# Attention with a token mixer: the value products of two steps in one burst, behind the eighth slot of a pair

## The chip, the cores and the metric

The kernel runs on one core of one Trainium2 chip. The metric is the device time of one execution in microseconds. The engines are named as the profile names them: PE (TensorE, matrix products; PEld is its load of the stationary operand), DVE (VectorE), ACT (ScalarE), POOL (GpSimd) and SP (SyncE, here a queue of transfers). PE writes into PSUM, which has eight banks; a bank holds 128 rows of 512 numbers. Each engine works its instructions off in the order of the program and waits, where it must, on semaphores.

## The reference

From one input x of 2048 tokens by 512 channels, normalised over the channels to xn, two branches are computed and joined:

```python
def _A_ref(x, wqkv, wo):
    H = 32; Dh = D // H                      # 32 heads of 16
    q, k, v = ...                            # x @ wqkv
    p = _softmax(einsum("bhqd,bhkd->bhqk", q, k) * Dh ** -0.5)
    return einsum("bhqk,bhkd->bhqd", p, v)...reshape(B, S, D) @ wo

def _B_ref(x, w1, b1, w2, b2):
    h = _layernorm(x)
    u = _gelu(einsum("bsd,sf->bdf", h, w1) + b1)     # F = 1792
    return (einsum("bdf,fs->bds", u, w2) + b2).transpose(0, 2, 1)

xn = _layernorm(x)
out = x + _A_ref(xn) * _silu(_B_ref(xn))
```

The softmax is over all 2048 keys, so for each of the 32 heads there are 2048 by 2048 scores, their row maxima, their exponentials and the products with the values.

## The kernel before, in words

A first part (to about 200 us of the span) normalises x, makes q, k and v and puts them away in device memory. Then comes the main loop, which this change is about.

**Steps.** The heads are taken in 16 pairs. For a pair of heads there are 32 steps of scores: a step `t` is one block of 128 keys against one span of 1024 queries, for both heads (`a` = 0 and 1, in rows 0 to 63 and 64 to 127 of PE) and both halves of the span, so four products of 512 columns (`score`, L750), each followed by an exponential on ACT that writes a `prob` tile (L762). The values of a step (`values`, L764) are four products with the `prob` tiles, which stand side by side in four column groups of PE; in the trace a step has eight instructions for them, all of L773. They add up in the one bank `av` over the 16 blocks of keys. When the last is done, `put_away` (L509) is put on a list: ACT copies `av` out and SP sends it away.

**Maxima.** The exponentials need the row maxima beforehand. So a second stream runs 20 steps ahead (`LEAD`): `max_of` (L378) multiplies 128 queries by 512 keys, and DVE reduces the bank to one column (L391). There are four such products a step as well, two for either head. Once in 16 steps the maxima are complete for a span; `max_rows` (L393) takes the negative, PE turns it (`turn`, L402), DVE and POOL copy it, and four transfers of POOL's queue write it into rows of q.

**The mixer.** The token mixer's matrix products (48 products of 512 columns for a tile of the first matrix, 42 for one of the second, all into the one bank `dn`) are fed in between. Each is cut into two halves of 64 rows (L911), so that a half runs beside a product of the attention in the other half of the rows. When a tile is complete, ACT reads `dn` (`gelu`, L459, or `silu`, L493), and the next tile may begin.

**Banks.** Three banks are for scores (`sc`), three for maxima (`mx`), one is `av`, one is `dn`.

**The order in a pair of steps.** The loop (L944) does two steps at a time, `s` and `s + 1`. It takes up to six products of the mixer and follows an order written out by hand (`ORDERS`, L892): two strings, one for either half of PE's rows, in which `m` is a maximum, `s` a score and `D` a half of a product of the mixer. Position i of the two strings is a slot: its two products run side by side. The strings have 8, 10, 12 or 14 slots, for 0, 2, 4 or 6 products of the mixer; this document calls that the kind of the pair. In kind 6 the maxima are in slots 0, 2, 4, 6, 7, 9, 11 and 13 and the scores in 1, 3, 5, 6, 7, 8, 10 and 12. The third entry of an order is the slot ahead of which the loop stops: there it turns the maxima if that is due, emits the values of step `t - 2` (L969), and works off the list of later work (`run_later`). The values of step `t - 1` are emitted after the last slot (L1020). So PE does two bursts of values in a pair: one in the middle, one between the pairs. A tile of the mixer that ends within a pair leaves a shorter take, and the next pair begins the next tile with kind 4.

**The list of later work.** `later` holds functions; `run_later` runs them all, at the top of a pair and at its middle; `after(n, f)` runs f at the n-th time.

**The tail.** After step 492 of the scores there are no maxima left, and PE does the output's products (L886) between the scores. For the last heads' first span, `own` (L606) makes two pieces of work for the side; the second, `move_in` (L641), divides the values and sends them by POOL's queue into rows of `oc`. From the block of tokens number eight on, `rest` (L781) waits for `own_done` before it emits a product that reads those rows (L816).

Of the kernel before, what the change touches and what calls it, by code (L numbers as in the profile page):

```python
# [21 lines left out]
def tile_attention_token_mixer(ctx, tc, x, wqkv, wo, w1, b1, w2, b2, out):  # L22
# [343 lines left out]
    def after(n, f):  # L366

        later.append(f if n == 1 else lambda: after(n - 1, f))
# [232 lines left out]


    asides = []
    own_done = [False]

    def own(span, ev):  # L606
        rq = sm.tile([P, 4, 4], F32, name="rq", bufs=1)
        wide = el.tile([P, 512], F32, name="t", bufs=4)

        def one(pl=ps_mx, nm="mx"):  # L610

            ps = pl.tile([P, 512], F32, name=nm)
            for k in range(4):
                at = slice(k * P, (k + 1) * P)
                nc.tensor.transpose(ps[:, at], ev[:, at], ident)
            turned = ps.rearrange("p (k j r) -> p k j r", k=4, j=4)
            for a in range(2):
                nc.vector.reciprocal(rq[:, :, 2 * a : 2 * a + 2], turned[:, :, 2 * a : 2 * a + 2, 16 - 16 * a])
            nc.vector.tensor_copy(
                wide.rearrange("p (k j r) -> p k j r", k=4, j=4), rq.unsqueeze(3).to_broadcast([P, 4, 4, 32]),  # L620
            )

        def two(pl=ps_mx, nm="mx"):

            ps = pl.tile([P, 512], F32, name=nm)
            for k in range(4):
                nc.tensor.matmul(
                    ps[:, k * P : (k + 1) * P], wide[:, k * P : (k + 1) * P], ident, start=True, stop=True,
                )
            return ps  # L630

        def chunk(ps, of, at):
            nc.vector.tensor_tensor(out=ev[:, at], in0=ps[:, at], in1=ev[:, at], op=OP.mult)
            nc.scalar.copy(of[:, 0, at], ev[:, at])
            sub(nc.vector, of[:, 1, at], ev[:, at], of[:, 0, at])

        if span == QH - 1:
            asides.extend((one, two, chunk))
            return

        def move_in():  # L641
            ps = two()
            of = el.tile([P, 2, 512], F32R, name="uo")
            chunk(ps, of, slice(0, 512))
            for a in range(2):
                for c in range(2):
                    row = 32 * (2 * a + c) + DH * a
                    move(oc[ND - 1, c][96 + DH * a : 112 + DH * a, :, :], of[row : row + DH, :, :], nc.gpsimd)
            own_done[0] = True

        asides.extend((one, move_in))


# [110 lines left out]
    def values(t):  # L764
        p, r = divmod(t, SPP)
        span, kb = divmod(r, NB)
        if kb == 0:
            state["av"] = ps_av.tile([P, 512], F32, name="av")
        av = state["av"]
        for a in range(2):  # L770
            for c in range(2):
                j = 2 * a + c
                nc.tensor.matmul(  # L773
                    av[32 * j : 32 * j + 32, :],
                    vps[p][:, kb, 16 * a : 16 * a + 32], prob.pop((t, a, c)),
                    start=kb == 0, stop=kb == NB - 1,
                )
        if kb == NB - 1:
            later.append(lambda: put_away(p, span, av))

    def rest():  # L781

        for n in range(N_W - 2, N_W):
            w_split(n)
        for b in range(2):
            load_part(b)

        def until(ready):
            while not ready():
                yield None  # L790

        def products(ps, b, groups, rows=None):
            at = slice(b % 4 * P, (b % 4 + 1) * P)
            for g in groups:
                o = oc[g, b // 4]
                at_g = rows if g == ND - 1 else None
                for j, (m, w) in enumerate(((0, whs), (0, wls), (1, whs))):
                    w = w[N_MIX + g].rearrange("p a b -> p (a b)")
                    yield (
                        ps, lambda r, o=o, m=m, s=at_g: o[s or r, m, at], lambda r, w=w, s=at_g: w[s or r, :],  # L800
                        g == groups[0] and j == 0, g == groups[-1] and j == 2,
                    )

        for b in range(PARTS):
            yield from until(lambda: all((g, b // (NB // QH)) in divided for g in range(ND - 1)))
            ps = ps_dn.tile([P, 512], F32, name="dn")[:, :D]
            yield from products(ps, b, range(ND - 1))
            yield lambda b=b, ps=ps: part(b, ps)
            yield None
        load_last_w()  # L810
        yield from until(lambda: now[0] >= NU and (ND - 1, QH - 1) in divided)
        for n in range(4):
            load_out(n)
        for n, b in enumerate(blocks):
            if n == NB // 2:
                yield from until(lambda: own_done[0] and (ND - 1, 0) in divided)  # L816
            ps = ps_dn.tile([P, 512], F32, name="dn")[:, :D]
            rows = slice(0, DH * heads_of(ND - 1) if n < NB // 2 else P)
            if b >= PARTS:
                yield from products(ps, b, range(ND), rows)  # L820
            else:
                yield from products(ps, b, [ND - 1], rows)
            yield lambda n=n, ps=ps: finish(n, ps)
            yield None
# [55 lines left out]
    def whole(x, then):  # L880
# [9 lines left out]


    ORDERS = {  # L892
        0: ("smsmsmsm", "msmsmsms", 3),
        2: ("smsmDDsmsm", "msmsmsmsDD", 3),
        4: ("sDDDDmsmsmsm", "msmsmsmDDDDs", 6),
        6: ("DDDDDDsmsmsmsm", "msmsmsmsDDDDDD", 7),
    }

    def halves(lead, n):
# [44 lines left out]
    for s in range(0, total + 1, 2):  # L944
# [8 lines left out]
        if s < NU and t >= 0:  # L953
            steady[0] = True
            late = ended[0]
            n = max(0, min(6, round((wanted(s + 1) - done) / 2) * 2))
            one, two, then = halves(lead, min(n, 4) if late else n)
            made = [dict(D=part, m=heads[a][0], s=heads[a][1]) for part, a in ((one, lead), (two, 1 - lead))]
            first, second, middle = ORDERS[(len(one) + 1) // 2 * 2]
            if one:  # L960
                lead = 1 - lead
            for i, kinds in enumerate(zip(first, second)):
                if i == middle:
                    now[0] = s + 1
                    if turn:
                        turn()
                        turn = None
                    if 0 <= t - 2 < NT:
                        values(t - 2)  # L969
                    run_later()  # L970
                for of, kind in zip(made, kinds):
                    if of[kind]:
                        of[kind].pop(0)()
                if "D" in kinds and not two:
                    for f in then:
                        f()
                    then = []
            for f in then:
                f()
        elif s < NU:  # L980

            for i in range(4):
                first_maxima.append((s + i // 2, i % 2))
                if len(first_maxima) == 3 or i == 3 and (s % 16 == 14 or s + 2 == LEAD):
                    for u, half in first_maxima:
                        max_of(u, half, 0)
                        max_of(u, half, 1, ps_sc, "sc")
                    first_maxima.clear()
                    take(EARLY, whole)
                if i == 1:  # L990
                    now[0] = s + 1
                    run_later()
        else:
            made = [heads[a][1] for a in range(2)]
            n = len(made[0])
            for i in range(n):
                made[1][i]()
                made[0][i]()
                if i == n - 2:
                    if turn:  # L1000
                        turn()
                        turn = None
                    elif asides:
                        asides.pop(0)()
                    values(t - 2)
                    take(3 * ND, whole)
                    now[0] = s + 1
                    run_later()
            if 0 <= t - 1 < NT and (t - 1, 0, 0) in prob:
                if n:  # L1010
                    values(t - 1)
                    if s == total - 2:
                        load_gates(NB // 2, NB - 2)
                    take(3 * ND, whole)
            if s == total - 6:
                split_last_w()
# [72 lines left out]
```

## Time and profile before

| | |
|---|---|
| median of three runs | 1706.81 us (1706.4 to 1709.35) |
| the profiled execution | 1709.11 us |
| its span, first to last instruction | 1707.3 us |
| PE, DVE, ACT, POOL busy | 98%, 83%, 70%, 33% of the span |
| mean granted clock of TensorE | 0.995 |

A busy PE in the profile isn't PE at its peak: products in different rows overlap in the records, and their ends are modelled. What counts is from where to where a group of instructions stands and what its weight load waited for. In a row of the timeline the first number is the start in us from the span's start, the second the duration of the row, then engine, line, operation, output and inputs, shapes and the number of instructions; in brackets the idle time of the engine just before, and what ended it. `issue` means that the profile shows nothing that was waited for. DVE's records overlap a little when it works without rest, so that its pace is the distance of the starts.

### The profile page before, as it was taken

The numbers are of one execution on the slowest core, as the hardware profiler recorded it, in microseconds if no ns is written. First come the engines' busy times: TensorE is split into PE (matmuls) and PEld (weight loads), VectorE is DVE, ScalarE is ACT, GpSimd is POOL, SyncE is SP. The second block draws the span as 40 slices with busy tenths as digits, with TensorE's granted clock in tenths as the row PEclk, the third lists the DMA queues.
The fourth block names the chain that finished last, engine by engine and source line by source line (L and its number), as shares of the span: only waits on it lengthen the run. The fifth ranks groups of instructions, "written<-read, shape, count | busy, mean of one in ns | idle before, by whom it ended". The sixth has DMA issues, their size and how long they took to land.

```text
span 1707.3 us, 30652 instructions
## 1 busy us (share of the span) xinstructions
PE 1672.8 (98%) x11716; PEld 846.9 (50%) x11716; DVE 1409.7 (83%) x2378; ACT 1187.9 (70%) x2291; POOL 567.1 (33%) x673
## 2 busy tenths in 40 slices
PE   7999999999999999999999999999999999999987
PEld 6887644444444444444444444444444444444443
DVE  6565888888888888888888888888888888888834
ACT  3333277777777777777777777777777777787845
POOL 4223842233342334333422322222222222463401
PEclk9999999999999999999999999999999999999999
DMA  6467611415150514353332415141515132272435
GB/s 222 179 235 184 133 44 42 75 44 85 45 85 20 92 46 68 135 127 94 75 60 64 79 35 82 36 80 31 81 33 82 37 48 52 78 158 85 147 98 186
DMA packets 150879, 152.94 MB, mean 90 GB/s; under 512 B 51452, under 2 KB 109820, under 8 KB 147660
## 3 DMA queue, kind: packets, MB, share of 16 engines
q1 hardware_dynamic: 146188, 149.97, 36.8%
q0 software_dynamic: 4544, 1.01, 0.4%
q8 instruction: 92, 1.51, 0.4%
q14 instruction: 55, 0.45, 0.1%
HBM read 100.29 MB, written 49.53 MB: 88 GB/s over the span
## 4 chain that ended last, share of the span: by engine, by line
PE 92%; DVE 5%; ACT 1%; DMA 0%; issue 0%; POOL 0%; SPq 0%; DVEq 0%; POOLq 0%
PE av L773 28%; PE dn L911 26%; PE mx L387 13%; PE sc L757 12%; DVE mxp L391 4%; PE dn L886 3%; PE mx L300 2%; PE sc L300 2%; ACT prob L762 1%; PE av L886 1%; PE av L300 1%; PE dn L300 1%; PE mx L757 1%; PE mx L402 0%; PE sc L83 0%
## 5 line engine op out<-in xcount | busy, mean ns | idle before, releaser
L391 DVE TENSOR_REDUCE mxp<-mx 128x1 f32<-128x512 f32 x2008 | 1250.5, 683 | 183.9 <-PE mx L387 97.4
L762 ACT ACTIVATE prob<-sc 128x512 f32<-128x512 f32 x2008 | 1041.8, 604 | 331.1 <-PE sc L757 252.6
L387 PE MATMUL mx<-big 48*128 48x512 f32 x2008 | 826.8, 428 | 2.1
L757 PE MATMUL sc<-big 50*128 50x512 f32 x2008 | 771.8, 428 | 3.4 <-DMA big<-m 2.0
L911 PE MATMUL dn<-hu,wh 64*128 64x512 f32 x1570 | 573.8, 406 | 0.0
L773 PE MATMUL av<-prob,vp 128*32 128x512 f32 x4096 | 546.3, 605 | 0.0
L387 PEld LDWEIGHTS mx<-big 48*128 48x128 f32 x2008 | 364.2, 186 | 221.8 <-DVE mxp L391 206.6
L757 PEld LDWEIGHTS sc<-big 50*128 50x128 f32 x2008 | 355.1, 185 | 191.7 <-ACT prob L762 173.3
L911 PEld LDWEIGHTS dn<-hu,wh 64*128 64x128 f32 x1570 | 289.3, 185 | 171.5 <-issue 145.5
L911 PE MATMUL dn<-hu,wl 64*128 64x512 f32 x786 | 316.3, 402 | 0.0
L145 POOL CAST wh<-raw 128x512 fp32r<-128x512 f32 x108 | 62.8, 582 | 327.3 <-PE dn L911 309.6
L76 POOL TENSOR_TENSOR wl<-raw,wh 128x512 fp32r<-128x512 f32 x124 | 150.3, 1215 | 38.6 <-ACT wh L147 29.9
L773 PEld LDWEIGHTS av<-prob,vp 128*32 128x32 f32 x4096 | 81.0, 108 | 150.6 <-issue 138.6
L911 PEld LDWEIGHTS dn<-hu,wl 64*128 64x128 f32 x786 | 145.9, 186 | 8.3 <-issue 0.8
L406 POOL CAST m<-f 16x128 fp32r<-16x128 f32 x32 | 9.0, 280 | 266.1 <-DVE f L405 266.1
L464 POOL TENSOR_TENSOR sq<-u 128x512 f32<-128x512 f32 x14 | 14.6, 1040 | 170.9 <-ACT u L463 170.9
L80 POOL DMA_DIRECT2D big<-m x128 | 67.7, 535 | 0.0
L762 ACT ACTIVATE prob<-mx 128x512 f32<-128x512 f32 x40 | 25.1, 627 | 29.2 <-PE sc L757 22.0
L500 POOL TENSOR_SCALAR t<-t 128x512 f32<-128x512 f32 x16 | 23.8, 1488 | 62.4 <-ACT t L497 62.4
L911 PE MATMUL dn<-wh,hu 64*128 64x512 f32 x120 | 41.6, 399 | 0.0
L76 POOL TENSOR_TENSOR hu<-hx,hu 128x512 fp32r<-128x512 f32 x16 | 20.4, 1291 | 54.6 <-ACT hu L243 54.6
L300 PE MATMUL mx<-xt,big 128*128 128x512 f32 x144 | 35.4, 395 | 0.0
(202 smaller groups left out, 1094.2 us busy)
## 6 DMA issues: line engine op xcount, KB each, us to landing
raw<-in_B_w_dram SPq DMA_DIRECT2D x104, 256.0 KB
big<-k_d SPq DMA_DIRECT2D x96, 128.0 KB
big<-q_d SPq DMA_DIRECT2D x96, 128.0 KB
q_d<-sg SPq DMA_DIRECT2D x16, 512.0 KB
k_d<-sg SPq DMA_DIRECT2D x16, 512.0 KB
num_d<-ev SPq DMA_DIRECT2D x30, 256.0 KB
u_d<-uo SPq DMA_DIRECT2D x14, 512.0 KB
hu<-u_d SPq DMA_DIRECT2D x14, 512.0 KB
```

Of the source, the lines that this page charges most:

```text
L76: eng.tensor_tensor(out=o, in0=a, in1=b.bitcast(F32), op=OP.subtract)
L80: queue.dma_start(dst.bitcast(F32), src.bitcast(F32))
L145: nc.gpsimd.tensor_copy(whs[n][:, :m, :], raws[n][:, :m, :])
L300: nc.tensor.matmul(ps, w[part][:, kd, m], xt[kd][:, z, :], start=w is wh and z == 0 and kd == 0, stop=w is wl and kd == ND - 1,)
L387: nc.tensor.matmul(ps, q[o : o + 48, r * P : (r + 1) * P], k[o : o + 48, c * 512 : (c + 1) * 512], start=True, stop=True,)
L391: nc.vector.tensor_reduce(mxp[u // 16][:, a, r % 8, c : c + 1], ps, axis=AX.X, op=OP.max)
L500: nc.gpsimd.tensor_scalar(t, t, 1.0, None, op0=OP.add)
L757: nc.tensor.matmul(ps, ks[p][o : o + 50, kb * P : (kb + 1) * P], qs[p][o : o + 50, at : at + 512], start=True, stop=True,)
L762: nc.scalar.activation(e, ps, AF.Exp, scale=scale)
L773: nc.tensor.matmul(av[32 * j : 32 * j + 32, :], vps[p][:, kb, 16 * a : 16 * a + 32], prob.pop((t, a, c)), start=kb == 0, stop=kb == NB - 1,)
L886: nc.tensor.matmul(ps, w(slice(0, P)), m(slice(0, P)), start=first, stop=last)
L911: made.append(lambda r=r, start=first and a == lead, stop=last and a != lead: nc.tensor.matmul(ps, w(r), m(r), start=start, stop=stop,))
```

## The change

The third entry of each order goes up by one, and at that place the values of both steps, `t - 2` and `t - 1`, are emitted on end; after the last slot nothing is left to emit. So in kind 6 the slots 0 to 7 come ahead of the burst and 8 to 13 behind it, in kind 4 0 to 6 and 7 to 11, in kinds 0 and 2 0 to 3 and the rest; the next pair's slots follow the last slot of this one without a burst between. The strings are the same, and so are the positions of maxima and scores. Both steps' `prob` tiles were made in the pair before, in the old order as in the new. The turning of the maxima stays ahead of the burst. Values that complete a span now put `put_away` on the list just before the list is worked off at the middle, not at the end of the pair.

A second part concerns the tail: `own_done` is no longer set when `move_in` has been emitted, but two turns of the list of later work after that.

```diff
     asides = []
-    own_done = [False]
+    own_done = []
...
                     move(oc[ND - 1, c][96 + DH * a : 112 + DH * a, :, :], of[row : row + DH, :, :], nc.gpsimd)
-            own_done[0] = True
+            after(2, lambda: own_done.append(True))
...
-                yield from until(lambda: own_done[0] and (ND - 1, 0) in divided)
+                yield from until(lambda: own_done and (ND - 1, 0) in divided)
...
     ORDERS = {
-        0: ("smsmsmsm", "msmsmsms", 3),
-        2: ("smsmDDsmsm", "msmsmsmsDD", 3),
-        4: ("sDDDDmsmsmsm", "msmsmsmDDDDs", 6),
-        6: ("DDDDDDsmsmsmsm", "msmsmsmsDDDDDD", 7),
+        0: ("smsmsmsm", "msmsmsms", 4),
+        2: ("smsmDDsmsm", "msmsmsmsDD", 4),
+        4: ("sDDDDmsmsmsm", "msmsmsmDDDDs", 7),
+        6: ("DDDDDDsmsmsmsm", "msmsmsmsDDDDDD", 8),
     }
...
-                    if 0 <= t - 2 < NT:
-                        values(t - 2)
+                    for v in (t - 2, t - 1):
+                        if 0 <= v < NT:
+                            values(v)
                     run_later()
```

## The prediction

> **What bounds the kernel now.** I read the page first, then the timeline of single pairs of steps. The page: the span, the granted clock in tenths over 40 slices, the chain that ended last, and the two groups that speak of the row maxima (busy us, mean ns of one, then idle time before them and who ended it).
>
> ```profile
> span 1707.3 us, 30652 instructions
> PEclk9999999999999999999999999999999999999999
> PE 92%; DVE 5%; ACT 1%; DMA 0%; issue 0%; POOL 0%; SPq 0%; DVEq 0%; POOLq 0%
> L391 DVE TENSOR_REDUCE mxp<-mx 128x1 f32<-128x512 f32 x2008 | 1250.5, 683 | 183.9 <-PE mx L387 97.4
> L387 PEld LDWEIGHTS mx<-big 48*128 48x128 f32 x2008 | 364.2, 186 | 221.8 <-DVE mxp L391 206.6
> ```
>
> The chain is PE's, but DVE's reductions of the maxima fill 1250.5 us, and PE's weight loads already stand 206.6 us for them: the second engine is close behind. The page can't say how close, since that is settled inside one pair. The next view sums the stretch from the first burst of value products to one near the end of the main loop, for the lines of the value products and of the turning of the maxima; the rows after it are single bursts.
>
> ```profile
> 214.47:1608.44 1393.97, 518.89 (x3896) 76.67 (x3896) 1.00 0.33 70
> 214.47:1608.44 1393.97, 8.31 (x30) 2.62 (x30) 1.00 0.33 70
> 217.38 1.06 PE L773 MATMUL av<-prob,vp 128*32 128x512 f32 x8
> 222.86 1.06 PE L773 MATMUL av<-prob,vp 128*32 128x512 f32 x8
> 280.06 1.07 PE L773 MATMUL av<-prob,vp 128*32 128x512 f32 x8
> 285.33 1.07 PE L773 MATMUL av<-prob,vp 128*32 128x512 f32 x8
> ```
>
> A step's values are 8 instructions, so 3896 are 487 bursts or 243.5 pairs, and a pair takes 1393.97 / 243.5 = 5.725 us, at a granted clock of 1.00. A pair of kind 4 takes 222.86 - 217.38 = 5.48, one of kind 2 takes 285.33 - 280.06 = 5.27. A pair of kind 6, the commonest, is in the timeline of the weight loads, DVE and ACT (start, duration, engine, line):
>
> ```profile
> 599.99 0.16 PEld L773 LDWEIGHTS av<-prob,vp 128*32 128x32 f32 x8 [0.25 <-issue]
> 601.33 0.18 PEld L911 LDWEIGHTS dn<-hu,wh 64*128 64x128 f32 x1
> 601.56 0.18 PEld L911 LDWEIGHTS dn<-hu,wh 64*128 64x128 f32 x1
> 601.79 2.07 ACT L762 ACTIVATE prob<-sc 128x512 f32<-128x512 f32 x4 [0.94 <-PE sc L757]
> 602.87 0.16 PEld L773 LDWEIGHTS av<-prob,vp 128*32 128x32 f32 x8 [0.24 <-issue]
> 603.86 0.18 PEld L387 LDWEIGHTS mx<-big 48*128 48x128 f32 x1 [0.84 <-DVE mxp L391]
> 604.40 2.48 DVE L391 TENSOR_REDUCE mxp<-mx 128x1 f32<-128x512 f32 x4 [0.31 <-PE sc L757]
> 605.75 0.16 PEld L773 LDWEIGHTS av<-prob,vp 128*32 128x32 f32 x8 [0.37 <-issue]
> ```
>
> From here come the constants: the kind 6 pair is 605.75 - 599.99 = 5.76; a burst holds PE 603.86 - 602.87 = 0.99; a maximum in the first slot behind a burst reaches DVE after 604.40 - 603.86 = 0.54, a product of the second slot its reader after 601.79 - (599.99 + 0.99) = 0.81; a slot costs 0.23 (601.33 to 601.56), the first behind a burst 0.11 more. Eight reductions at 0.60 ((2.48 - 0.68) / 3 from start to start) are 4.8 of 5.76 us: DVE idles 0.96 a pair, in two rests of about half a microsecond, one at each burst.
>
> How maxima back up when more of them stand between two bursts is in the trace too: in kind 0 the second stretch has five. Its weight loads, and DVE beside them in two windows:
>
> ```profile
> 1606.14 0.18 PEld L387 LDWEIGHTS mx<-big 48*128 48x128 f32 x1 [0.84 <-DVE mxp L391]
> 1606.76 0.18 PEld L387 LDWEIGHTS mx<-big 48*128 48x128 f32 x1 [0.33 <-DVE mxp L391]
> 1607.42 0.18 PEld L387 LDWEIGHTS mx<-big 48*128 48x128 f32 x1
> 1608.02 0.18 PEld L387 LDWEIGHTS mx<-big 48*128 48x128 f32 x1 [0.41 <-DVE mxp L391]
> 1608.44 0.16 PEld L773 LDWEIGHTS av<-prob,vp 128*32 128x32 f32 x8 [0.24 <-issue]
> 1605.43 4.32 DVE L391 TENSOR_REDUCE mxp<-mx 128x1 f32<-128x512 f32 x7
> 1605.43 1.94 DVE L391 TENSOR_REDUCE mxp<-mx 128x1 f32<-128x512 f32 x3
> ```
>
> Five slots take 1608.44 - 1606.14 = 2.30 us instead of 5 x 0.23 + 0.11 + 0.19 = 1.45. With three mx buffers a product waits until the third one before it is reduced: the reduction ends at 1605.43 + 1.94 = 1607.37 and the load follows at 1607.42, 0.05 later. And the burst stands behind the last maximum in PE's queue, at 0.42 after its load.
>
> **The change, step by step.**
>
> *Two bursts become one.* The same 16 instructions a pair. The price of two steps on end is in the only place where steps follow each other now, near the end:
>
> ```profile
> 1685.72 0.13 PEld L773 LDWEIGHTS av<-prob,vp 128*32 128x32 f32 x4 [0.30 <-issue]
> 1686.15 0.13 PEld L773 LDWEIGHTS av<-prob,vp 128*32 128x32 f32 x4 [0.30 <-issue]
> ```
>
> Half a step every 0.43, so a second step adds 0.86 and a double burst holds PE 0.99 + 0.86 = 1.85. Saved on PE a pair: 0.13 of the second burst's end, 0.11 of its first slot, 0.42 - 0.23 = 0.19 before it: 0.43. Were PE the only limit this were 243.5 x 0.43 = 105 us.
>
> *The maxima stand still for longer.* Let zero be the start of the first reduction after the burst. DVE has eight to do until the next burst ends; the slots bring them faster (0.47 for two slots) than 0.60, so it runs without rest. The fifth starts at 2.40, ends at 3.08; the eighth product (the last before the burst in every kind) loads at 3.13, the burst at 3.55, ends at 5.40. In kind 6 the next maximum is in the second slot behind it, so DVE starts at 5.40 + 0.81 = 6.21; in kinds 0, 2 and 4 in the first: 5.94. DVE is done with the eighth at 4.8, so it rests 1.4 in kind 6 where it rested 0.96. So +0.45 for kind 6, +0.46 for kind 4, +0.67 for kind 2. Scores have the same three buffers, but ACT's start to start is (2.07 - 0.60) / 3 = 0.49: never last here, taken as 0.
>
> *The turning of the maxima*, once in eight pairs, keeps its place ahead of the burst, one slot later, and takes an mx buffer as well:
>
> ```profile
> 608.65 0.09 PEld L402 LDWEIGHTS mx<-ident,neg 128*16 128x16 f32 x1 [0.28 <-DVE mxp L391]
> 608.86 0.16 PEld L773 LDWEIGHTS av<-prob,vp 128*32 128x32 f32 x8
> ```
>
> It now waits for the sixth reduction instead of following the fourth product: 0.60 after the eighth's load (plus 0.2 for the short reduction ahead of it), then 0.21 to the burst (608.65 to 608.86). The burst comes at 0.60 + 0.20 + 0.21 - 0.42 = 0.6 later. Ends: 0, if DVE's work hides in its rest, and 0.6; I take 0.6 since PE itself stands. The four row transfers from POOL's queue move by the same, and have a pair and a half until they are read: nothing.
>
> *A cover that goes.* A tile of the mixer ends with a pair of kind 2 and the next begins with kind 4, in the only dn buffer. ACT must have read it before the second slot of the next pair, and the burst between the pairs gave it time:
>
> ```profile
> 336.96 0.18 PEld L911 LDWEIGHTS dn<-hu,wl 64*128 64x128 f32 x1
> 338.05 0.73 ACT L463 ACTIVATE u<-dn,b1t 128x512 f32<-128x512 f32 x1
> 338.89 0.18 PEld L911 LDWEIGHTS dn<-hu,wh 64*128 64x128 f32 x1 [0.25 <-issue]
> ```
>
> Even now the load waits 0.25. Without the burst: ACT begins the first of four scores 0.81 behind the burst's end, reads dn at 0.81 + 4 x 0.49 = 2.77, until 3.50; the load comes 0.11 later, at 3.61, where the slots would be there by about 2.3. The next maximum is one slot on and reaches DVE at 3.61 + 0.81 = 4.42, where it was due at 0.54 + 5 x 0.60 = 3.54. So about 0.8 a tile. Ends: 0 and 1.3; 0.8 is DVE's own loss.
>
> *Put away and later work.* The values of a span's last step now come before the list of later work instead of after the pair: ACT's copy of av and SP's transfers go out half a pair sooner, and the next span's first value product has a whole pair for it: 0. Nothing is queued behind a new semaphore on SP or POOL.
>
> *The tail.* The last heads' blocks now begin two turns of the list after their rows have been sent. Now PE stands at the first of them:
>
> ```profile
> 1651.34 1.07 PE L773 MATMUL av<-prob,vp 128*32 128x512 f32 x8
> 1657.55 0.77 PE L886 MATMUL dn<-wh,hu 128*128 128x512 f32 x1 [5.14 <-DMA hu<-uo]
> 1659.83 1.93 PE L773 MATMUL av<-prob,vp 128*32 128x512 f32 x8
> 207.49 0.50 PE L911 MATMUL dn<-hu,wh 64*128 64x512 f32 x1
> 209.63 0.77 PE L911 MATMUL dn<-hu,wh 64*128 64x512 f32 x1
> ```
>
> PE would do one slot, a burst, three slots and a burst more (0.42 + 0.99 + 0.9 + 0.99 = 3.3 us) before it asks for the rows at 1657.55: 3.3 less standing, and some of the slower stretch behind it (a burst of 1.93 instead of 1.07) may go. Ends 0 and -8; I take -5. A wait of 2 us or so can still slow the matmuls: the first ones after the pause at 205 to 207.49 take 0.50, two microseconds later one takes 0.77.
>
> [...]
>
> *The sum.* A mixer tile of 48 products is one pair of kind 4, seven of kind 6 and one of kind 2 (4 + 42 + 2). It takes 7 x 6.21 + 2 x 5.94 + 0.8 + 9/8 x 0.6 = 56.8, that is 6.31 a pair; with six of kind 6 it comes to the same. 243.5 x (6.31 - 5.725) = +142; with the tail +137. The profiled execution took 1709.11 with a span of 1707.3, 2.3 over the median of 1706.81. So 1846 for it and 1844 for the median.
>
> How far these steps can be trusted: worked over half a pair of before, they give, for kind 6, 0.81 + 0.60 + 0.05 for the fourth score's buffer, then 0.42 and 0.99, 2.87 against 605.75 - 602.87 = 2.88 measured; the other kinds come within 0.1 a pair. 0.1 a pair is 24 us.
>
> **Rivals.**
> *PE alone counts, and it is faster.* It decides if the eighth product need not wait: if DVE took under about 0.45 from start to start, or the buffers were five. Then -105 - 5: 1597. For it: the chain is 92% PE. Against: the five-maxima stretch above, where exactly this wait is seen at 0.60.
> *The two cancel.* DVE would rest 0.96 a pair as now, the tail gain is left: 1702. It would need the rests of the two bursts simply to add up; but what hides a burst is three buffers' work, 1.8 us, and that is had once a pair then, not twice.
> *The clock falls.* PE stands about 0.3 in each of the last slots before the burst, every pair. If the granted clock then halved for half of the time, a pair would cost some 0.9 more (a burst of 1.93 for 1.07 and slots alike): 1844 + 220 = 2060. Against: stands of 0.2 in every half pair now, and a clock of 1.00. [...]
> *Slower, but by less.* Turns and tile ends hidden and the recurrence 0.1 or more too long: below 1780.
>
> **How the numbers follow.** As worked 0.80, slower by less 0.07, the clock 0.06, faster 0.05, cancelling 0.02. The likeliest gives 1844. Its low end takes away 24 for the recurrence, 27 tiles x 0.8 = 22, 30 turns x 0.6 = 18: 1780. The high end adds 24 and takes no gain in the tail: 1873, with the later dn read (27 x 0.5 more) 1880. 0.2%, 3.4 us, is about what a measurement of this kernel tells from no change (its runs lie 3 us apart): faster 0.05, same 0.02, slower 0.93.
>
> **What would show it.** Bursts of 16 value products every 6.2 us in kind 6 and 5.9 elsewhere; 1.85 from a burst's first load to the next slot's; weight loads of the maxima before the burst each standing for L391 and 0.6 apart; one rest of DVE a pair, of 1.3 to 1.4; the load of dn standing over 1 us at tile ends; clock 1.00. Wrong if the burst starts without a wait for DVE, or if DVE's reductions speed up; in the tail, if PE stands for hu<-uo as long as before.

## The result, and the profile after

The changed kernel takes 1878.4 us (1875.1 to 1880.7) where the kernel before takes 1707.9, a ratio of 1.0997 with a 95% interval of 1.0975 to 1.102. The profiled execution took 1876.81 with a span of 1875.0. The forecast was 1844, between 1780 and 1880: the direction and the wait for DVE are right, the time is 34 us too low. That it still lies below the upper end is in part luck: the range made room for a less exact working, no gain in the tail and a later read of dn, and not for the fall of the clock at tile ends, which the runs below show.

First the page of the changed kernel: the span, the chain that ended last, and the two groups that speak of the maxima.

```profile
span 1875.0 us, 30654 instructions
PE 57%; DVE 35%; ACT 5%; issue 1%; DMA 1%; SPq 0%; POOL 0%; DVEq 0%; ACTq 0%; POOLq 0%
L391 DVE TENSOR_REDUCE mxp<-mx 128x1 f32<-128x512 f32 x2008 | 1233.8, 683 | 375.0 <-PE dn L911 218.7
L387 PEld LDWEIGHTS mx<-big 48*128 48x128 f32 x2008 | 372.5, 187 | 298.8 <-DVE mxp L391 250.6
```

DVE's share of the chain went from 5% to 35%, although DVE does the same 2008 reductions and is less busy as a share (74% of the span for 83%). Its idle time went from 183.9 to 375.0 us: this is not an engine with more work, but one that rests while PE does the double burst and that PE must then wait for. The stretch of the main loop from the first burst to one near its end, with the sums of the value products (L773), has the price of a pair:

```profile
214.63:1775.23 1560.60, 482.87 (x3888) 103.67 (x3888) 0.98 0.30 63
```

3888 instructions are 243 pairs: 6.422 us each, against 5.725 before. The stretch is the whole loss, and the column before the DMA share is the granted clock: 0.98, where it was 1.00. The first I had worked out; a falling clock I had given as a rival with a chance of 6%, but for another reason and of another size (2060).

One pair of kind 6 after, PE's weight loads and DVE (the loads that show a wait, and the bursts):

```profile
613.62 0.16 PEld L773 LDWEIGHTS av<-prob,vp 128*32 128x32 f32 x8 [0.25 <-issue]
615.47 0.18 PEld L757 LDWEIGHTS sc<-big 50*128 50x128 f32 x1 [0.84 <-issue]
...
618.18 0.18 PEld L387 LDWEIGHTS mx<-big 48*128 48x128 f32 x1 [0.30 <-DVE mxp L391]
...
618.78 0.18 PEld L387 LDWEIGHTS mx<-big 48*128 48x128 f32 x1 [0.18 <-DVE mxp L391]
619.37 0.18 PEld L387 LDWEIGHTS mx<-big 48*128 48x128 f32 x1 [0.41 <-DVE mxp L391]
...
619.81 0.16 PEld L773 LDWEIGHTS av<-prob,vp 128*32 128x32 f32 x8 [0.25 <-issue]
616.24 4.88 DVE L391 TENSOR_REDUCE mxp<-mx 128x1 f32<-128x512 f32 x8 [1.32 <-PE dn L911]
```

The pair is 619.81 - 613.62 = 6.19 (forecast 6.21); the burst holds PE 1.85 (1.85); the last maxima's loads stand 0.60 apart, each for L391; the eighth loads at 619.37, 3.13 behind the first reduction's start at 616.24 (3.13); DVE has one rest, 1.32 in the records (1.3 to 1.4). Before, a pair had two rests, of 0.31 to 0.43 each in the records of 600 to 620 us where no turn came between.

Then a tile end of the mixer after, as PE's bursts, ACT's read of dn, and the weight load that waits for it:

```profile
463.72 1.92 PE L773 MATMUL av<-prob,vp 128*32 128x512 f32 x16
468.30 0.71 ACT L463 ACTIVATE u<-dn,b1t 128x512 f32<-128x512 f32 x1
469.12 0.18 PEld L911 LDWEIGHTS dn<-hu,wh 64*128 64x128 f32 x1 [1.43 <-issue]
471.39 2.93 PE L773 MATMUL av<-prob,vp 128*32 128x512 f32 x16
470.10:473.50 3.40, 3.40 (x19) 1.25 (x20) 2.31 (x4) 1.80 (x4) 3.15 (x5) 0.50 0.10 27
```

The load of dn comes at 469.12, 3.55 behind the burst's end at 465.57 (forecast 3.61), after a stand of 1.43. But the next burst takes 2.93 instead of 1.92, and the last row, a window of its own, has the reason: from 470.10 on the granted clock is 0.50 for 3.40 us. The stand I had foreseen, at this place; the fall of the clock behind it I had not.

The tail did what was expected of it. In the chain of waits of before PE stood 5.14 us for the rows of the last heads; now

```profile
1830.39 0.47 PE L886 MATMUL dn<-wh,hu 128*128 128x512 f32 x1 [1.83 <-DMA hu<-uo]
1831.68 1.69 PE L773 MATMUL av<-prob,vp 128*32 128x512 f32 x8
```

it stands 1.83, and the burst behind it still takes 1.69; the granted clock is 0.50 from 1832.0 to 1835.4.

### The profile page after: what moved, and what is told of

It is laid out like the page before. It is cut to its first block, busy times and chain, and to the rows that moved or that the text cites. A ratio compares the mean times of both kernels' runs of the same rounds, so it can differ in the third digit from the quotient of the medians.

```text
span 1875.0 us, 30654 instructions
## 1 busy us (share of the span) xinstructions
PE 1774.9 (95%) x11716; PEld 951.2 (51%) x11716; DVE 1393.1 (74%) x2378; ACT 1224.0 (65%) x2291; POOL 567.8 (30%) x673
## 4 chain that ended last, share of the span: by engine, by line
PE 57%; DVE 35%; ACT 5%; issue 1%; DMA 1%; SPq 0%; POOL 0%; DVEq 0%; ACTq 0%; POOLq 0%
DVE mxp L391 34%; PE av L773 26%; PE mx L387 9%; PE sc L757 6%; ACT prob L762 4%; PE dn L911 4%; PE dn L886 3%; PE mx L300 2%; PE sc L300 2%; PE av L886 1%; ACT ev L496 1%; PE av L300 1%; PE dn L300 1%; PE mx L757 1%; PE mx L402 0%
## 5 line engine op out<-in xcount | busy, mean ns | idle before, releaser
L391 DVE TENSOR_REDUCE mxp<-mx 128x1 f32<-128x512 f32 x2008 | 1233.8, 683 | 375.0 <-PE dn L911 218.7
L762 ACT ACTIVATE prob<-sc 128x512 f32<-128x512 f32 x2008 | 1080.9, 600 | 434.7 <-PE dn L911 272.1
L387 PE MATMUL mx<-big 48*128 48x512 f32 x2008 | 863.1, 458 | 28.1 <-DVE mxp L391 2.1
L757 PE MATMUL sc<-big 50*128 50x512 f32 x2008 | 763.3, 429 | 10.2 <-ACT prob L762 8.2
L911 PE MATMUL dn<-hu,wh 64*128 64x512 f32 x1570 | 583.0, 426 | 27.9 <-ACT ev L496 16.2
L387 PEld LDWEIGHTS mx<-big 48*128 48x128 f32 x2008 | 372.5, 187 | 298.8 <-DVE mxp L391 250.6
L773 PE MATMUL av<-prob,vp 128*32 128x512 f32 x4096 | 512.2, 617 | 0.0
L757 PEld LDWEIGHTS sc<-big 50*128 50x128 f32 x2008 | 363.5, 188 | 209.2 <-issue 142.7
L773 PEld LDWEIGHTS av<-prob,vp 128*32 128x32 f32 x4096 | 108.5, 112 | 225.2 <-issue 220.2
L512 ACT COPY ev<-av 128x512 f32<-128x512 f32 x32 | 18.8, 587 | 41.9 <-PE av L773 41.9
```

Source lines behind the costliest of these rows:

```text
L387: nc.tensor.matmul(ps, q[o : o + 48, r * P : (r + 1) * P], k[o : o + 48, c * 512 : (c + 1) * 512], start=True, stop=True,)
L391: nc.vector.tensor_reduce(mxp[u // 16][:, a, r % 8, c : c + 1], ps, axis=AX.X, op=OP.max)
L757: nc.tensor.matmul(ps, ks[p][o : o + 50, kb * P : (kb + 1) * P], qs[p][o : o + 50, at : at + 512], start=True, stop=True,)
L762: nc.scalar.activation(e, ps, AF.Exp, scale=scale)
L773: nc.tensor.matmul(av[32 * j : 32 * j + 32, :], vps[p][:, kb, 16 * a : 16 * a + 32], prob.pop((t, a, c)), start=kb == 0, stop=kb == NB - 1,)
L911: made.append(lambda r=r, start=first and a == lead, stop=last and a != lead: nc.tensor.matmul(ps, w(r), m(r), start=start, stop=stop,))
```

## The experiments

My theory was that of the banks: three `mx` buffers hold 1.8 us of DVE's work (three reductions at 0.60), a double burst with what surrounds it takes longer, so DVE rests once a pair and PE then waits for it ahead of the next burst. Rivals were that a burst of sixteen is dear in itself, that PE alone counts, and, for the part I had undersized, that tile ends or the clock cost more than I had worked out.

In the rows that follow, each a window from the first burst to one near the end of the main loop for L773, the first number is the stretch in us, then PE's busy time with the count, PEld's, and the granted clock. 3888 instructions are 243 pairs with double bursts, 3896 are 487 single bursts or 243.5 pairs.

**The tail alone.**

```diff
-            own_done[0] = True
+            after(2, lambda: own_done.append(True))
```

(and its two readers), all else as before.

> The kernel before with the second part of the change alone: own_done set two turns of the list later. In the trace of the change the tail from the first burst of the last steps to the end took 1875.0 - 1789.0 = 86.0 us, before it took 1707.3 - 1616.2 = 91.1. If the tail part acts by itself: 1707 - 5 = 1702, ratio 0.997, with PE waiting some 1.8 us instead of 5.1 for the rows of hu from uo. If the shorter tail came from the main loop's other timing: 1707, ratio 1.000.

Measured: 1701.45 us, ratio 0.9965 (0.9951 to 0.9979). So the second part of the change is a gain of 6 us on its own, and the first part costs about 177. The wait for the rows is 1.88 here, and the clock stays whole:

```profile
1656.48 0.47 PE L886 MATMUL dn<-wh,hu 128*128 128x512 f32 x1 [1.88 <-DMA hu<-uo]
1656.50:1663.50 7.00, 7.00 (x43) 2.73 (x43) 3.70 (x6) 4.41 (x9) 0.00 (x0) 1.00 0.33 93
```

**Reductions over half the columns**, in the changed kernel. Half of the keys is left out of the maxima, and the scale is smaller.

```diff
-        nc.vector.tensor_reduce(mxp[u // 16][:, a, r % 8, c : c + 1], ps, axis=AX.X, op=OP.max)
+        nc.vector.tensor_reduce(mxp[u // 16][:, a, r % 8, c : c + 1], ps[:, :256], axis=AX.X, op=OP.max)
...
-        nc.scalar.activation(e, ps, AF.Exp, scale=scale)
+        nc.scalar.activation(e, ps, AF.Exp, scale=scale / 16)
```

> The changed kernel, but each reduction of a maximum reads 256 of the 512 columns (the other half of the keys is left out of the maxima, and the exponentials are scaled down so that they stay finite), so that DVE's pace goes from 0.60 to about 0.33 us. Theory of the banks (PE waits at the last maxima before the burst because three buffers empty at 0.60 each): the wait for L391 before the burst goes, a pair of kind 6 falls from 6.19 to about 5.6, where PE and ACT's three buffers are the next limit; 1720 to 1745 in all, with the slow clock behind tile ends still there. Theory of the burst (sixteen value products on end are dear in themselves, whatever DVE does): a pair stays at 6.1 to 6.2 and the time above 1850.

Measured: 1733.7, ratio 1.018 (1.0135 to 1.023). A pair of kind 6 and the average pair (1419.62 / 243 = 5.842):

```profile
609.05 0.16 PEld L773 LDWEIGHTS av<-prob,vp 128*32 128x32 f32 x8
613.74 0.18 PEld L757 LDWEIGHTS sc<-big 50*128 50x128 f32 x1 [0.20 <-ACT prob L762]
614.65 0.16 PEld L773 LDWEIGHTS av<-prob,vp 128*32 128x32 f32 x8 [0.25 <-issue]
212.15:1631.77 1419.62, 477.54 (x3888) 102.98 (x3888) 0.99 0.32 69
```

The pair is 614.65 - 609.05 = 5.60, as expected; no load of it waits for DVE any more, two wait for ACT (the other at 614.22). Shorter reductions (763 us in this stretch for 1191), with nothing of PE's work changed, take 145 us away; some 12 of these are an estimate for the clock, which falls for 9 stretches of 3.41 us here instead of 20 (priced below at 1.14 each). The burst theory falls, that of the banks stands. The time is still above that of before, although this pair is shorter than the 5.76 of before. The tile ends are dearer: the pair over one takes 7.12 (487.41 to 494.53 in its trace, with a whole clock), and PE's load of dn stands 1.43 in it, as in the changed kernel.

**The control: the same reductions in the kernel before.**

> The kernel before with the reductions over 256 of 512 columns and the exponentials scaled down, as in e2_half_reduce: the control to it. Theory of the banks: before, a half pair of kind 6 is set by the fourth score's buffer (ACT), not by DVE, so a pair stays at 5.75 and only the stretches with five maxima in kinds 0 and 2 get shorter, by about 0.4 each: 1707 - 11 = 1696. If DVE's pace were what sets the pairs of before as well: below 1650.

Measured: 1698.75, ratio 0.9952 (0.9936 to 0.9969), and 1384.73 / 243.5 = 5.687 a pair. The kernel before hardly knows how fast DVE is; the changed one does.

```profile
214.06:1598.79 1384.73, 518.88 (x3896) 76.62 (x3896) 1.00 0.33 71
```

**Both readers quick**, in the changed kernel and in the kernel before. The exponentials cover 256 of 512 columns and the value products read these twice, besides the halved reductions: half of the keys is left out of the maxima, and half of the queries' exponentials stand in for the others.

```diff
-        nc.scalar.activation(e, ps, AF.Exp, scale=scale)
+        nc.scalar.activation(e[:, :256], ps[:, :256], AF.Exp, scale=scale / 16)
...
-                    vps[p][:, kb, 16 * a : 16 * a + 32], prob.pop((t, a, c)),
+                    vps[p][:, kb, 16 * a : 16 * a + 32], prob.pop((t, a, c))[:, :256].unsqueeze(1).to_broadcast([P, 2, 256]),
```

> The changed kernel with the reductions over 256 of 512 columns and the exponentials over 256 of 512 too (the value products read those 256 twice, so that PE's work is unchanged; half of the keys is left out of the maxima, and half of the queries' exponentials are put in the place of the others'). It takes both readers of the banks away as limits. If one burst a pair saves PE what the prediction worked out (0.43 a pair) and the readers alone took it back: kind 6 falls to 5.41 us, a tile's pairs to 5.45 on average, 1707 - 72 - 5 = 1630. If merging the bursts saves PE nothing: kind 6 stays at 5.6 or more, as with the reductions alone, and the time above 1700.

> The kernel before with reductions and exponentials over 256 columns, as in e6_half_both (1637.6): the control to it. With both readers quick PE sets the pair of two bursts. By the steps of the prediction (0.34 + 6 x 0.235 + 0.40 and 0.99 in each half) kind 6 takes 5.7 and kind 4 about 5.35, 1690 to 1700 in all, and the merged burst of e6_half_both saves some 55 to 60 us against it. If quick readers alone explain the 1637.6: about 1640 here too.

Measured: 1637.6 after (0.9592, 0.9579 to 0.9605) and 1663.3 before (0.9747, 0.9732 to 0.9761). A pair of kind 6 of the changed order, then of the order of before, then the two loops:

```profile
603.72 1.92 PE L773 MATMUL av<-prob,vp 128*32 128x512 f32 x16
609.07 1.92 PE L773 MATMUL av<-prob,vp 128*32 128x512 f32 x16
```

```profile
604.91 1.07 PE L773 MATMUL av<-prob,vp 128*32 128x512 f32 x8
610.56 1.06 PE L773 MATMUL av<-prob,vp 128*32 128x512 f32 x8
```

```profile
213.49:1541.03 1327.54, 468.86 (x3888) 101.59 (x3888) 1.00 0.35 74
```

```profile
212.87:1564.15 1351.28, 518.86 (x3896) 76.62 (x3896) 1.00 0.34 72
```

With quick readers a pair of kind 6 is 5.35 with one burst and 5.65 with two. So merging does save PE time, 0.30 a pair in kind 6, and over all kinds 5.549 - 5.463 = 0.09 a pair: 26 us between the two kernels, the tail's 6 among them. That is less than half of the 55 to 60 I had expected. The control came out at 1663 and not at 1690 to 1700: kind 6 is as expected (5.65 for 5.7, though the terms written down there add up to 6.28 and not to 5.7), but in the order of before a pair of kind 4 got shorter than expected, 5.20 (332.20 to 337.40 in its trace) for 5.35. What else the gain lacks lies at the tile ends, as the two traces show. From the last burst of kind 6 in one tile to the first in the next, three pairs, it takes 1170.19 - 1153.68 = 16.51 with one burst, 0.46 more than three pairs of 5.35; with two bursts, between the same places, 1145.79 - 1129.89 = 15.90, 1.05 less than three of 5.65. With one burst PE's load of dn stands 1.14 there (at 1163.24).

**A tile's end under the burst.** Only the order of kind 2 is another, so that the burst stands between the tile's last product and the next tile.

```diff
-        2: ("smsmDDsmsm", "msmsmsmsDD", 4),
+        2: ("DDsmsmsmsm", "msmsDDmsms", 6),
```

> The changed kernel, with another order for kind 2 alone: the last products of a mixer tile come in slots 0, 1 and 4, 5 and the burst ahead of slot 6, so that ACT reads dn while PE does the burst. Kind 6 stays as it is. Theory of the tile end (what the prediction undersized: at a tile end PE stands for ACT's read of dn, and the clock falls to half for 3.4 us after it): the pair over a tile end falls from 7.5 to 8.4 us to about 6.5, the granted clock stays at 1.00 in the main loop, and the time falls by 20 for the standing and some 20 for the clock, to 1836. If the clock falls for another reason (the waits before every burst): about 1858, with the clock still near 0.98. If neither matters: 1878.

Measured: 1838.3, ratio 1.0769 (1.0754 to 1.0783): 40 us less than the changed kernel, as the theory of the tile end has it. Bursts around a tile end, and the loop:

```profile
508.97 1.92 PE L773 MATMUL av<-prob,vp 128*32 128x512 f32 x16
514.56 1.92 PE L773 MATMUL av<-prob,vp 128*32 128x512 f32 x16
521.14 1.92 PE L773 MATMUL av<-prob,vp 128*32 128x512 f32 x16
215.41:1740.72 1525.31, 474.79 (x3888) 102.32 (x3889) 0.99 0.30 64
```

The pair over the end is 521.14 - 514.56 = 6.58 instead of 471.39 - 463.72 = 7.67, and the one after it has a whole clock. Kind 6 is unchanged, 6.19, with the same waits before every burst (0.18 to 0.42 each in the four loads ahead of the one at 621.18). So it is not these short waits that bring the clock down here. It is not quite the 1.00 expected: the trace's record of the granted clock still has 5 stretches of 3.41 us at half in this window, where the changed kernel has 20, and four of the five come after 1600 us, where the short tiles of the output begin.

**The burst at the end of a pair.** The turn and the list stay at the middle.

```diff
-                    for v in (t - 2, t - 1):
-                        if 0 <= v < NT:
-                            values(v)
                     run_later()
```

> The changed kernel, with the one burst of both steps moved from the middle to the end of a pair; the turning of the maxima and the list of later work stay at the middle. In all kinds a maximum is then in the first slot behind the burst, and a burst stands between a tile's end and the next tile. Theory of the banks: every kind takes 5.94, with the turns 6.01 a pair, no wait at tile ends and a clock of 1.00: 1707 + 64 - 5 = 1766. If what costs is the burst of sixteen as such, a pair stays at 6.2: 1815 or more. If PE alone counted: below 1707.

Measured: 1786.35, ratio 1.046 (1.0446 to 1.0474).

```profile
603.78 1.92 PE L773 MATMUL av<-prob,vp 128*32 128x512 f32 x16
609.77 1.92 PE L773 MATMUL av<-prob,vp 128*32 128x512 f32 x16
216.83:1686.51 1469.68, 467.48 (x3888) 101.41 (x3888) 1.00 0.31 67
```

A pair is 609.77 - 603.78 = 5.99 (expected 5.94) and 6.048 with the turns (6.01). The same two-step burst, 16 products on end, costs 92 us less at this place: a maximum stands in the first slot behind it, and it covers the tile ends. Of the 20 us over the expected 1766, some 9 are the 0.04 by which a pair is over 6.01, and 5 are a slip of mine: 243.5 x (6.01 - 5.725) is 69 and not 64. Another 4 are the distance of the profiled execution, 1782.2, from the median. The turns cost no more than I had allowed: the pair with one takes 634.19 - 627.73 = 6.46, 0.47 more than its neighbours.

**Kind 6 with its burst ahead of slot 7**, one number in the order.

```diff
-        6: ("DDDDDDsmsmsmsm", "msmsmsmsDDDDDD", 8),
+        6: ("DDDDDDsmsmsmsm", "msmsmsmsDDDDDD", 7),
```

> The changed kernel with the burst of kind 6 ahead of slot 7, where the middle burst of before was, instead of slot 8; the other kinds as changed. The first maximum then stands in the first slot behind the burst, not in the second. Theory of the banks: kind 6 goes from 6.19 to 5.94, 0.2 a pair on average, 1878 - 48 = 1830, with the clock falling at tile ends as before. If the place does not matter: 1878.

Measured: 1842.9, ratio 1.0806 (1.0782 to 1.0829).

```profile
598.85 1.92 PE L773 MATMUL av<-prob,vp 128*32 128x512 f32 x16
604.81 1.92 PE L773 MATMUL av<-prob,vp 128*32 128x512 f32 x16
214.25:1749.28 1535.03, 494.20 (x3888) 104.30 (x3888) 0.97 0.30 64
```

The pair is 5.96: one slot between the burst and the next maximum was worth 0.23. The clock is lower still, 0.97, but this execution took 1852.1, 9 us over the median; the other three, at 1840.7 to 1844.2, had 0.974 to 0.976 over the whole span, where the changed kernel's had 0.975 to 0.979. So the clock explains a small part at most of the 13 us by which the median is over the expected 1830; the rest stays open.

**The new places, but two bursts.**

```diff
-                    for v in (t - 2, t - 1):
-                        if 0 <= v < NT:
-                            values(v)
+                    if 0 <= t - 2 < NT:
+                        values(t - 2)
                     run_later()
```

> The changed kernel with the new places of the middle burst but two bursts again: the values of the first step there, those of the second after the last slot. So five maxima stand in one stretch and three in the other. Theory of the banks: the stretch with five waits for DVE, a pair of kind 6 takes 2.68 + 3.36 = 6.04 instead of 5.75, no long wait at tile ends, 1707 + 69 - 5 = 1771; that is, the uneven split alone costs about as much as the merged burst put at the end of a pair. If only the merging costs: 1702.

Measured: 1762.4, ratio 1.0329 (1.0314 to 1.0345). The stretches with three and with five maxima, and the load that waits in the long one:

```profile
642.80 0.16 PEld L773 LDWEIGHTS av<-prob,vp 128*32 128x32 f32 x8 [0.25 <-issue]
645.40 0.16 PEld L773 LDWEIGHTS av<-prob,vp 128*32 128x32 f32 x8 [0.37 <-issue]
648.31 0.18 PEld L387 LDWEIGHTS mx<-big 48*128 48x128 f32 x1 [0.27 <-DVE mxp L391]
648.77 0.16 PEld L773 LDWEIGHTS av<-prob,vp 128*32 128x32 f32 x8 [0.25 <-issue]
213.27:1667.00 1453.73, 518.86 (x3896) 76.63 (x3896) 1.00 0.32 67
```

The stretch with three maxima takes 645.40 - 642.80 = 2.60, that with five 648.77 - 645.40 = 3.37, and its last maximum waits for DVE: 5.97 a pair where it was 5.76 (expected 6.04), and 1453.73 / 243.5 = 5.970 over all kinds. Moving the middle burst by one slot, with nothing merged, already costs 61 us against the tail alone: the even split of the maxima around the two bursts was worth that.

**The tail with four turns instead of two.**

> The kernel before with own_done set four turns of the list later instead of at once (two turns gave 1701.5). If what is left of the wait for the rows (1.8 us at two turns) is the tail's only loss: 1700, with no wait for hu from uo. If the blocks of tokens that come later then pile up behind the last scores: 1702 to 1704.

Measured: 1701.3, ratio 0.9964 (0.9952 to 0.9977), no wait for the rows in its trace, and no gain over two turns. Part of what PE no longer stands for there it stands for later: its wait for DVE's L619 is 1.52 (at 1681.84), where with two turns it is 0.83 (at 1683.17), and the granted clock is 0.51 from 1683.40 to 1686.80. Whether this is the whole account stays open.

## Why the prediction was right, and where it was short

- *DVE paces the pair through three buffers.* Right, with its numbers: 6.19 for 6.21 in kind 6, the loads 0.60 apart, the eighth at 3.13. Shown by shortening the reductions in both kernels: 145 us after, 8 before. No run gives `mx` a fourth buffer: the kernel shares out eight banks as three, three, one and one. From the burst of a kind 4 pair to the next one it takes 5.96 where the clock is whole (1288.38 to 1294.34 below), for 5.94.
- *The first maximum one slot later in kind 6.* Right: 0.23 measured with the burst ahead of slot 7, 0.27 in the sum.
- *The turning of the maxima, 0.6.* Right: the pair with a turn is

```profile
607.41 0.16 PEld L773 LDWEIGHTS av<-prob,vp 128*32 128x32 f32 x8
600.59 0.16 PEld L773 LDWEIGHTS av<-prob,vp 128*32 128x32 f32 x8 [0.24 <-issue]
```

  607.41 - 600.59 = 6.82, beside 613.62 - 607.41 = 6.21 for the next one without.
- *The cover that goes at a tile's end.* The place, the reason and the stand were right. What I had at nothing is the clock behind the stand: I gave 0.8 a tile, 22 us in all, and put the fall of the clock down as a rival, and for another place (the short waits before every burst). The clock falls within 2 us behind 17 of the 26 stands of over 1.1 us that the load of dn has in the loop. Two ends of the same shape, 52 us apart, show the price of it: the bursts around each, and the clock in the window behind the first and around the second.

```profile
1229.14 1.92 PE L773 MATMUL av<-prob,vp 128*32 128x512 f32 x16
1237.52 2.17 PE L773 MATMUL av<-prob,vp 128*32 128x512 f32 x16
1243.72 1.92 PE L773 MATMUL av<-prob,vp 128*32 128x512 f32 x16
1231.00:1234.60 3.60, 2.22 (x19) 1.23 (x15) 3.04 (x5) 2.79 (x6) 0.00 (x0) 1.00 0.00 0
1234.70:1238.00 3.30, 3.30 (x16) 2.44 (x20) 1.92 (x4) 2.79 (x6) 2.74 (x3) 0.50 0.02 5
1280.90 1.92 PE L773 MATMUL av<-prob,vp 128*32 128x512 f32 x16
1288.38 1.92 PE L773 MATMUL av<-prob,vp 128*32 128x512 f32 x16
1294.34 1.92 PE L773 MATMUL av<-prob,vp 128*32 128x512 f32 x16
1283.00:1290.00 7.00, 5.62 (x42) 2.77 (x40) 5.57 (x9) 5.71 (x11) 2.97 (x3) 1.00 0.00 0
```

  The pair takes 8.38 us with the clock at half and 7.48 without, and the pair behind it, which the slow stretch reaches into, 6.20 and 5.96: the fall costs 14.58 - 13.44 = 1.14. By the steps of the prediction the first of them (nine maxima instead of eight) should be 5.94 + 0.60 + 0.8 = 7.34; the stand cost 0.14 more than I took, and 0.08 of that I had lost on paper, where 4.42 - 3.54 is 0.88 and not 0.8. Where the clock is whole, the sum holds: a tile of six pairs of kind 6, one each of kinds 4 and 2, and one turn is 6 x 6.21 + 2 x 5.94 + 0.8 + 0.6 = 50.54 by it, and from 1280.90 to the same burst of the next tile at 1331.52 it took 50.62. The stand is 1.43 at both (the loads of dn come at 1234.54 and 1286.31). Removing the stand in the order of kind 2 gave 40 us back. That agrees with an estimate of 41 from these rows: 7.48 - 6.58 = 0.9 at each of 27 tile ends, and 1.14 for each of the 15 stretches at half that went.
- *What is left.* A pair came out at 6.422 and not 6.31, 27 of the 34 us. Most of it is the clock: the trace's record of the granted clock has 20 stretches of 3.41 us at half in the main loop's window, none of them in the kernel before, and at 1.14 each that is an estimate of 23 us. How the rest divides between the ends of the output's short tiles of nine products and others stays open.
- *The range.* Its upper end does not come out of its terms: 1873 and 27 x 0.5 more is some 1886, not 1880. The result lies below either.
- *The tail, -5.* Right: -6 alone. That a wait near 2 us can still slow the matmuls was right after the change (a burst of 1.69 behind a stand of 1.83) and not in the tail alone (a clock of 1.00 behind a stand of 1.88).
- *The rival "PE alone counts", 1597.* It fell, and its price was wrong as well: PE's saving is 0.30 in kind 6 and not 0.43. The 0.13 of the burst's end is right; the step that failed is the 0.11 + 0.19 = 0.30 for a second stretch of slots. With quick readers seven slots take 607.74 - 605.90 = 1.84 from their first load to the burst, and fourteen 609.07 - 605.57 = 3.50, so that one stretch in place of two saves 2 x 1.84 - 3.50 = 0.18. The 0.11 was misread: before, the loads of the first three slots behind a burst stand at 600.99, 601.10 and 601.33, so the second comes sooner than after 0.23, and not later.
- *The clock as a rival.* The waits of 0.2 to 0.4 before every burst did not lower the clock here: with the burst at the pair's end there are such waits as well (0.19 to 0.31 ahead of the one at 609.77), and the clock is 1.00. It fell behind 17 of the 26 stands at tile ends, most of them of 1.43; with the other order of kind 2 there are 5 stretches at half instead of 20.

## What to carry to other kernels

Before two bursts on one engine are joined to save its switching, count the buffers between it and the engines that read its results: what they hold, times the reader's pace, must last for the whole joint burst and the way in and out, or the reader rests and the writer waits for it later: here they held 1.8 us, the burst alone took 1.85, and DVE rested 1.32 a pair. Look also at what a burst hides by standing where it stands: here the read of the mixer's bank cost a stand of 0.25 with a burst between two tiles (338.89 in the trace of before) and of 1.43 without (469.12 after). And a change of two parts is worth taking apart: the kernel before with the tail part alone, 1701.45 us, beats both, the one before by 6 us.

## What the runs showed that I had not expected

Behind a stand of PE of 1.43 us the granted clock went to half and stayed there for 3.41 us (from 1234.65 on): PE was busy for 2.22 of the 3.60 us before this fall. Behind the same stand 52 us later it stayed whole. In the first half of the loop the clock fell at nearly every tile end, in the second at every other one: the tiles there take some 51 us (1237.52 to 1288.38), and the falls in the record of the granted clock are 102.4 us apart. In the first half, where a tile takes 58.0 (463.72 to 521.73), most of them are 58.03 apart. What decides whether the clock falls behind a stand, no run shows. So the same place of the order was slow at one tile end and whole at the next, with 1.14 us between them.
